# Reordering the last tiles and the four quads of the first up-projection

## The chip, the cores and the metric

The kernel runs on one core of one Trainium2 chip. The metric is the time of one execution on the device in microseconds (us). Five engines of the core take part: PE (TensorE, matrix products), DVE (VectorE), ACT (ScalarE), POOL (GpSimd) and SP (SyncE, which issues nearly all the DMAs). Each works through its own instructions strictly in the order in which they were written, and waits at an instruction until its operands and its destination are free.

## What is computed

A chunked attention with a small memory feeds two feed-forward layers. In the reference, cut to what matters:

```python
def _attn_ref(q, k, v, mem_k, mem_v):          # per chunk of 32 queries, 16 left, 8 right, 8 memory slots
    scores = scale * np.matmul(q_c, k_full.transpose(0, 1, 3, 2))
    ...
    out[:, :, c_start:c_end] = np.matmul(a, v_full)

def _moe_ref(x, w_in, w_out, s, b):            # x: 3072 x 512, w_in: 512 x 2048, w_out: 2048 x 512
    h = x @ w_in
    r = np.maximum(h, 0.0)
    g = s * (r * r) + b
    return g @ w_out

def _moe2_ref(x, w_in, w_out):
    h = x @ w_in
    g = h - np.tanh(h)
    return g @ w_out
```

The change lies in the attention and in `h = x @ w_in` of the first layer ("up 1").

## The kernel before

Every product of two matrices is made of three matmuls, since both operands are split into an upper part (rounded, made by ACT) and a lower part (the rest, made by DVE): upper by upper on L238, lower weights by upper tokens on L239, upper weights by lower tokens on L240. A matmul has 128 x 128 weights and 512 columns.

The tokens stand in six blocks of 512. The work on them goes through these stages:

- **The list** (`START`): attention and the first 36 tiles of up 1, written out by hand as tokens of a letter and a number. `F` is a tile's products (12 matmuls of 512 columns), `r` its relu on ACT, which reads the bank of PSUM, `Q` its square into the group's tile `oa` (on ACT for tiles in `SCALAR_SQUARES`, else on DVE, where it also reads the bank). Tiles share three banks in turn, so tile n+3 can't start before `r` or `Q` of tile n has read its bank. Four tiles are a group; `k` and `K` form its differences in the tile `ob` on DVE (two instructions each), `st` stores `oa` and then `ob` (L621, L622). There are two pairs of `oa` and `ob`, so a group writes into the tiles of the group before the last, once their stores have landed.
- Beside them stand the conversions of the second layer's weights, piece by piece (numbers 0 to 7): `wl` load (1 MB, into the tile `raw`), `ws` scaled on ACT (L245), `wf` filled on DVE (L251, L255), `wd` store, `wc` four sums on DVE (L964, L892), `ww` their store, which frees `raw`. `wr` 4 to 7 (`w1_sums`) form sums of the weights of up 1 for the quads (five instructions on DVE and a store).
- **The plain run**: tiles 36 to 79, with the last units of attention in bursts. `P2_STEPS` places conversions among them, `QUADRANTS` those of the first down-projection's weights (load at the tile that is the key; `begin` on ACT and `end` on DVE at the two tiles in the value), `EXTRAS` the preparation of the quads: `t_sum` and `t_split` form sums of token blocks and split them, `ws_load` and `ws_split` fetch and split the weights' sums.
- **Four quads**: the last two blocks of tokens are done with seven products in place of eight. Each quad has the products P1 to P7 of six matmuls, in three banks. In the code, PE's order is P6, P2, P5, P1 of the next quad, P3, P7 of the next quad, P4. Between products that add up in one bank, ACT copies the bank's state out (`copy`), so P5 waits for `copy(2)` and P3 for `copy(3)`. `add` (DVE) forms three of the four results, `square` squares them, `combos` forms four differences (DVE) and stores. P7, P6, P5 and P3 use the split sums of weights `ws`, P7 first.
- **The first down-projection** (`down1.run`): its entries of 12 matmuls take parts that are loaded from the stores above and split by ACT (L761) and DVE (L762) into the ring.

SP's queue of DMAs holds up all that stand behind a DMA which waits: for its source, or for the tile that it overwrites. The queue's order is that of the code.

Of the kernel before, what the change touches and what calls it, by code (L numbers as in the profile page):

```python
# [27 lines left out]
NB = 512  # L28
# [123 lines left out]
def tile_chunk_attention_two_ffn(  # L152
# [11 lines left out]
    nc = tc.nc  # L164
# [94 lines left out]
    def filled_in_raw(z, raw):  # L259
# [13 lines left out]
    A_T = {"T3": "E0", "T2": "E1", "T1": ("Z2", "Z3"), "T4": ("Z4", "Q2")}  # L273
    A_WORDS, A_WS = ("Z0", "Z1", "Q1", "Q0"), ("E2", "E11", "E4", "E5")
# [17 lines left out]
    Z2 = {("A11", 0): ("E14", 0), ("A11", 1): ("E14", 1), ("A21", 0): "Z0", ("A21", 1): "Z1",  # L292
          ("A22", 0): "Z7", ("A22", 1): "Z8", ("A12", 0): "Z9", ("A12", 1): "Z10"}
# [210 lines left out]
    full = {}  # L504
# [386 lines left out]
    def minus(out, x, y):  # L891
        nc.vector.tensor_tensor(out=out, in0=x, in1=y, op=ALU.subtract)  # L892
# [111 lines left out]
    for token in START.split():  # L1004
        name = token.rstrip("0123456789")
# [86 lines left out]
    class UpQuad:  # L1092
# [57 lines left out]
        def combos(self):  # L1150
            combine(*(t.rearrange("p s b t -> p s (b t)") for t in (self.oa, self.ob)), nc.vector)
# [8 lines left out]
    q = upq[0]  # L1160
# [2 lines left out]
    q.mult("P7")  # L1163
    for s, q in enumerate(upq):
        p, r = upq[s - 1] if s else None, upq[s + 1] if s + 1 < QUADS else None
        q.mult("P6")
        if p:
            p.add(3)
        q.copy(2)
        if s == 0:  # L1170
            t_split("T4")
            ws_load(3)
        if p:
            p.square(3)
        q.mult("P2")
        q.add(1)
        if s == 3:
            down1.weights(0, 0)
        q.square(1)
        if p:  # L1180
            p.combos()
        else:
            up1_combine(21, None)
            up1_store(21)
        if s == 0:
            quads[0].begin()
            quads.append(down1.load_quadrant("E8"))
        if s == 1:
            quads.pop(0).end()
        if s == 2:  # L1190
            quads.pop(0).end()
            down1.load_to(0)
        q.mult("P5")
        q.copy(3)
        q.add(2)
# [208 lines left out]
    q = quads2[0]  # L1404
# [210 lines left out]
```

## Time and profile before

| | |
|---|---|
| time, median of 3 runs | 1059.72 us (1058.91 to 1062.29) |
| the profiled execution's own time | 1061.24 us |
| its span from first to last instruction | 1059.4 us (1.84 us lie around it) |
| PE busy | 1021.9 us, 96% of the span |
| DVE, ACT busy | 809.6 us (76%), 598.7 us (57%) |
| TensorE's granted clock, mean | 0.99 of full speed |
| moved by DMA | 273.12 MB, 258 GB/s |

Times in rows are counted from the span's start. A row's "idle before" is the time for which its engine stood before this instruction, with what ended the wait behind the arrow. PE's matmuls overlap: a busy PE is not a PE at its peak, and the distance between two starts is what one matmul costs.

### The profile page before, as it was taken

Reading aid. Unit: us, or ns where it says so; the run is one execution under the profiler, and the core shown is the slowest. Engines: PE = TensorE matmul, PEld = TensorE weight load, DVE = VectorE, ACT = ScalarE, POOL = GpSimd, SP = SyncE. Lnnn points to the kernel's source line nnn. Section 1 sums busy time; section 2 is a strip of 40 time slices with the busy share of each in tenths; the row PEclk is TensorE's granted clock in tenths of the full one; section 3 lists DMA queues with packets and bytes.
Section 4 is the critical chain, followed back from the end, with each engine's and each line's share of the span. In section 5 each row is a group of like instructions: output and inputs, shape, how many; then the busy total and the mean of one; then the engine's idle time right before and its main releaser. Section 6 shows DMA issues by size and latency. Waiting matters only on the chain.

```text
span 1059.4 us, 15630 instructions
## 1 busy us (share of the span) xinstructions
PE 1021.9 (96%) x6088; PEld 841.5 (79%) x6088; DVE 809.6 (76%) x993; ACT 598.7 (57%) x1098; POOL 12.6 (1%) x53
## 2 busy tenths in 40 slices
PE   7999969999998789999999999999999999999998
PEld 5888758888876568888888888888888888888887
DVE  7998865787566688889878788888888976776654
ACT  8998626657654466566655554454445564444442
POOL 1000000000000000000000000000000000000000
PEclk9999989999998999999999999999999999999999
DMA  8898696898855699787664146665568995556671
GB/s 339 305 329 315 236 405 271 329 343 299 321 217 213 211 382 348 255 313 261 210 200 158 41 189 238 248 239 218 218 249 321 351 375 186 191 189 243 231 264 60
DMA packets 85930, 273.12 MB, mean 258 GB/s; under 512 B 5984, under 2 KB 13408, under 8 KB 75104
## 3 DMA queue, kind: packets, MB, share of 16 engines
q1 hardware_dynamic: 85856, 272.13, 70.0%
q8 instruction: 47, 0.77, 0.3%
q14 instruction: 27, 0.22, 0.1%
HBM read 163.06 MB, written 109.05 MB: 257 GB/s over the span
## 4 chain that ended last, share of the span: by engine, by line
PE 86%; DVE 6%; DMA 3%; ACT 3%; issue 1%; SPq 1%; DVEq 0%; ACTq 0%
PE pb L238 28%; PE pb L239 27%; PE pb L240 27%; DVE ob L626 2%; PE pb L480 1%; DMA o<-oa 1%; PE pb L371 1%; PE pb L443 1%; DMA v<-in_vw_dram 1%; DVE sm L394 1%; DMA qk<-in_qk_dram 1%; DMA part<-o 1%; ACT sm L412 1%; DVE sm L427 0%; ACT r L600 0%
## 5 line engine op out<-in xcount | busy, mean ns | idle before, releaser
L240 PE MATMUL pb<-ringhringl,whl 128*128 128x512 f32 (+1 forms) x680 | 263.2, 387 | 3.4 <-DVE ringhringl L762 3.4
L238 PE MATMUL pb<-ringhringl,whl 128*128 128x512 f32 (+1 forms) x680 | 263.1, 387 | 1.6 <-ACT ringhringl L761 1.6
L239 PE MATMUL pb<-ringhringl,whl 128*128 128x512 f32 (+1 forms) x680 | 262.9, 387 | 0.0
L766 ACT ACTIVATE ringhringl<-part 128x1024 fp32r<-128x1024 f32 x120 | 127.0, 1060 | 148.9 <-PE pb L240 145.7
L767 DVE TENSOR_TENSOR ringhringl<-part,ringhringl 128x1024 fp32r<-128x1024 f32 x120 | 146.8, 1223 | 73.2 <-ACT ringhringl L766 73.0
L240 PEld LDWEIGHTS pb<-ringhringl,whl 128*128 128x128 f32 x680 | 127.7, 188 | 30.1 <-DVE ringhringl L762 4.7
L238 PEld LDWEIGHTS pb<-ringhringl,whl 128*128 128x128 f32 x680 | 127.7, 188 | 28.3 <-ACT ringhringl L761 2.4
L239 PEld LDWEIGHTS pb<-ringhringl,whl 128*128 128x128 f32 x680 | 127.7, 188 | 26.1
L238 PE MATMUL pb<-xh,w 128*128 128x512 f32 (+1 forms) x344 | 135.8, 395 | 9.1 <-DVE oa L614 8.7
L239 PE MATMUL pb<-xh,w 128*128 128x512 f32 (+1 forms) x344 | 133.4, 388 | 0.1
L240 PE MATMUL pb<-xl,w 128*128 128x512 f32 (+1 forms) x344 | 133.3, 387 | 0.0
L239 PE MATMUL pb<-x2hx2l,w 128*128 128x512 f32 x224 | 87.1, 389 | 0.0
L238 PE MATMUL pb<-x2hx2l,w 128*128 128x512 f32 x224 | 87.1, 389 | 0.0
L240 PE MATMUL pb<-x2hx2l,w 128*128 128x512 f32 x224 | 87.1, 389 | 0.0
L238 PEld LDWEIGHTS pb<-xh,w 128*128 128x128 f32 x344 | 65.3, 190 | 25.4 <-DVE oa L614 10.3
L761 ACT ACTIVATE ringhringl<-part,b_c 128x1024 fp32r<-128x1024 f32 x48 | 54.9, 1149 | 38.0 <-PE pb L240 28.4
L600 ACT ACTIVATE r<-pb 128x512 f32<-128x512 f32 x80 | 47.1, 595 | 51.7 <-PE pb L240 50.7
L240 PEld LDWEIGHTS pb<-xl,w 128*128 128x128 f32 x344 | 65.2, 190 | 13.3
L239 PEld LDWEIGHTS pb<-xh,w 128*128 128x128 f32 x344 | 65.3, 190 | 12.7 <-DVE w L570 0.3
L1367 ACT ACTIVATE pb<-oa 128x512 f32<-128x512 f32 x72 | 43.2, 599 | 53.8 <-DVE oa L1359 52.8
L762 DVE SCALAR_TENSOR_TENSOR ringhringl<-part,b_c,ringhringl 128x1024 fp32r<-128x1024 f32 x48 | 61.4, 1282 | 15.6 <-ACT ringhringl L761 15.5
L412 ACT ACTIVATE sm<-sm,nmx 128x96 f32<-128x96 f32 x192 | 69.1, 368 | 4.0 <-DVE nmx L404 4.0
(177 smaller groups left out, 1501.9 us busy)
## 6 DMA issues: line engine op xcount, KB each, us to landing
part<-o SPq DMA_DIRECT2D x84, 512.0 KB, 5.3
part<-o SPq DMA_DIRECT2D x42, 1024.0 KB, 5.9
o<-oa SPq DMA_DIRECT2D x24, 1024.0 KB, 3.9
o<-ob SPq DMA_DIRECT2D x20, 1024.0 KB, 5.8
o<-ob SPq DMA_DIRECT2D x24, 768.0 KB, 5.3
raw<-in_wi_dram SPq DMA_DIRECT2D x16, 1024.0 KB, 6.7
raw<-in_wo_dram SPq DMA_DIRECT2D x16, 1024.0 KB, 8.7
o<-oa SPq DMA_DIRECT2D x20, 768.0 KB, 5.8
```

The source lines that it names most:

```text
L238: nc.tensor.matmul(acc, lhsT=whi, rhs=xhi, start=first, stop=False, skip_group_check=more)
L239: nc.tensor.matmul(acc, lhsT=wlo, rhs=xhi, start=False, stop=False, skip_group_check=more)
L240: nc.tensor.matmul(acc, lhsT=whi, rhs=xlo, start=False, stop=last, skip_group_check=more)
L371: nc.tensor.matmul(score_bank(u, g)[QE * e:QE * (e + 1), KE * (r0 + r):KE * (r0 + r + 1)], lhsT=tq[sl, r, QE * e:QE * (e + 1)], rhs=tk[sl, ...
L412: nc.scalar.activation(out=sm[:, h, :], in_=sm[:, h, :], func=AF.Exp, bias=nmx[:, h:h + 1], scale=1.0, **({"accum_out": sums[:, h:h + 1]} ...
L600: nc.scalar.activation(out=r, in_=up_ps[p], func=AF.Relu)
L626: sub = lambda o, x, y: eng.tensor_tensor(out=o, in0=x, in1=y, op=ALU.subtract)
L761: nc.scalar.activation(out=xh, in_=src, func=AF.Identity, bias=self.bias)
L762: nc.vector.scalar_tensor_tensor(out=xl, in0=src, scalar=self.bias, in1=xh.bitcast(F32), op0=ALU.add, op1=ALU.subtract)
L766: nc.scalar.activation(out=xh, in_=src, func=AF.Copy)
L767: nc.vector.tensor_tensor(out=xl, in0=src, in1=xh.bitcast(F32), op=ALU.subtract)
L1367: nc.scalar.activation(out=self.rs[o], in_=src, func=AF.Tanh)
```

## The change

Three places change; no matmul is added, removed or moved.

**In the list**, the conversion of piece 3 and the sums `wr6` and `wr7` leave it: piece 3 goes to tiles 42 to 50 of the plain run (the later pieces move up to 8 tiles back), the sums to tiles 38 and 41. The steps of piece 0 move to later places in the list. **At the end of the plain run**, the sums of tokens T2 and T4 get tiles of their own and are formed earlier. **In the quads**, splitting the weights is cut in two: the upper part is made before `copy(2)`, the lower part right behind `add(1)`; `combos` is cut in halves, one ahead of P2 and one behind `add(2)`; the conversion (`end`) comes last; square 2 goes from one instruction on DVE to two on ACT. The last quad splits the down-projection's weights at these places, and loads three parts two quads earlier.

```diff
-wr4 r19 r21 F20 ws0 F24 Q19 wr5 r20 E14 F22 r22 qk16 D12 st3 Q20 wf0 wd0 F23 r23 wr6 Q21 ws2 F25 k4
-Q22 wc0 ww0 F26 wl3 Q23 wf2 wd2 K4 r24 r26 F27 st4 D14 k5 r25 K5 Q24 wc2 ww2 F28 Q25 wr7 Q26 ws3 r27
-F29 st5 Q27 wf3 wd3 F30 r29 r28 Q29 wc3 ww3 k6 K6 r30 st6 Q28 F31 F32 X13 Q30 r31 L13 T12 T14 Q31
-r32 k7 K7 Q32 F35 r35 F34 Q35 C12 r34 F33 vv12 Q34 r33 st7 S16 V12 Q33 k8 K8 st8 X12 M16 L12 R16 C14
+wr4 r19 r21 F20 F24 Q19 wr5 r20 E14 F22 r22 qk16 D12 st3 Q20 F23 r23 Q21 ws2 F25 k4 Q22 F26 ws0 Q23
+wf2 K4 r24 r26 F27 wd2 st4 D14 k5 r25 K5 Q24 wc2 F28 Q25 Q26 r27 F29 ww2 st5 Q27 F30 r29 r28 Q29 k6
+K6 r30 st6 Q28 F31 F32 X13 Q30 r31 L13 T12 T14 Q31 r32 k7 K7 Q32 F35 r35 F34 Q35 C12 r34 F33 vv12
+Q34 wf0 r33 st7 wc0 S16 V12 Q33 k8 K8 wd0 ww0 st8 X12 M16 L12 R16 C14
...
-for m, at in ((4, (42, 45, 46, 50)), (5, (50, 53, 54, 58)), (6, (58, 60, 61, 64)), (7, (66, 68, 69, 72))):
+for m, at in ((3, (42, 45, 46, 50)), (4, (50, 53, 54, 57)), (5, (57, 60, 61, 64)), (6, (64, 67, 68, 71)),
+              (7, (71, 74, 75, 78))):
...
     EXTRAS = {
-        71: [(ws_load, 0), (ws_load, 1)], 72: [(t_sum, "T3")], 74: [(t_split, "T3")], 75: [(t_sum, "T2")],
-        76: [(t_split, "T2")], 77: [(t_sum, "T1"), (t_split, "T1")], 78: [(ws_split, 0), (ws_load, 2)],
-        79: [(t_sum, "T4")],
+        38: [(w1_sums, 6)], 41: [(w1_sums, 7)],
+        71: [(ws_load, 0), (ws_load, 1), (t_sum, "T3"), (t_sum, "T2")], 72: [(t_sum, "T1"), (t_split, "T1")],
+        73: [(t_sum, "T4"), (ws_load, 2)], 74: [(t_split, "T3")], 76: [(t_split, "T2")],
+        77: [(t_split, "T4"), (ws_load, 3)], 78: [(ws_high, 0), (ws_low, 0)],
     }
...
-            if o in (0, 1):
+            if o != 3:
                 nc.scalar.activation(out=t, in_=t if o else self.acc(0), func=AF.Relu)
...
         q.mult("P6")
         if p:
             p.add(3)
+            p.square(3)
+        if r:
+            ws_high(s + 1)
         q.copy(2)
...
-        if p:
-            p.square(3)
-        q.mult("P2")
-        q.add(1)
...
         if p:
-            p.combos()
+            p.combos(0)
...
+        q.mult("P2")
+        q.add(1)
...
+        if r:
+            ws_low(s + 1)
+        else:
+            down1.low(0, 0)
+        q.mult("P5")
+        q.copy(3)
+        q.square(1)
+        q.add(2)
+        if p:
+            p.combos(1)
...
-        if r:
-            ws_split(s + 1)
-            r.mult("P1")
-            r.copy(1)
...
         q.mult("P3")
-        q.square(2)
         q.square(0)
-        if s == 1:
-            quads[0].begin()
+        if s in (1, 2):
+            quads.pop(0).end()
...
         if r:
             r.mult("P7")
+        q.square(2)
```

On SP's queue, near the list's end, before (`ws` are the sums of up 1's weights, `w2z` the converted weights, `raw` a load, `o1` the groups' stores):

```order
L981 DMA w1s_5_88<-ws_1706 128x1024
L340 DMA qk_1738<-in_qk_dram 128x1152
L621 DMA o1_0_73<-oa_1426 128x1536
L622 DMA o1_0_73<-ob_1427 128x2048
L958 DMA w2z_0_91<-zw_1691 128x1024
L981 DMA w1s_6_89<-ws_1766 128x1024
L970 DMA w2z_0_91<-raw_1468 128x1024
L544 DMA raw_1808<-in_wi2_dram 128x2048
L958 DMA w2z_2_93<-zw_1774 128x1024
L621 DMA o1_1_74<-oa_1662 128x1536
```

and now, at the same place:

```order
L982 DMA w1s_5_88<-ws_1704 128x1024
L341 DMA qk_1736<-in_qk_dram 128x1152
L622 DMA o1_0_73<-oa_1426 128x1536
L623 DMA o1_0_73<-ob_1427 128x2048
L959 DMA w2z_2_93<-zw_1762 128x1024
L622 DMA o1_1_74<-oa_1662 128x1536
```

Four DMAs between the stores of group 3 (`o1_0_73`) and group 4 (`o1_1_74`) are gone.

On DVE, in the second quad, before (`keep` to `oa` is an `add`, `oa` to `oa` a square, `ob` the differences, `zq` the conversion, `ws` the weights' lower part):

```order
L1140 TENSOR_TENSOR oa_3590<-keep_3556,pb_69 128x2x256
L1148 SCALAR_TENSOR_TENSOR oa_3590<-oa_3590 128x2x256
L1140 TENSOR_TENSOR oa_3659<-keep_3555,pb_69 128x2x256
L626 TENSOR_TENSOR ob_3591<-oa_3590 128x512
L626 TENSOR_TENSOR ob_3591<-oa_3590,ob_3591 128x512
L626 TENSOR_TENSOR ob_3591<-oa_3590 128x512
L626 TENSOR_TENSOR ob_3591<-ob_3591,oa_3590 128x512
L251 TENSOR_SCALAR zq_3601<-zq_3601 128x1024
L255 SCALAR_TENSOR_TENSOR zq_3601<-raw_3449,zq_3601 128x1024
L1140 TENSOR_TENSOR oa_3659<-oa_3659,pb_69 128x2x256
L892 TENSOR_TENSOR ws_3682<-words_3536,ws_3682 128x1024
L1148 SCALAR_TENSOR_TENSOR oa_3659<-oa_3659 128x2x256
```

and now:

```order
L1146 TENSOR_TENSOR oa_3600<-keep_3564,pb_69 128x2x256
L1154 SCALAR_TENSOR_TENSOR oa_3600<-oa_3600 128x2x256
L627 TENSOR_TENSOR ob_3601<-oa_3600 128x512
L627 TENSOR_TENSOR ob_3601<-oa_3600,ob_3601 128x512
L1146 TENSOR_TENSOR oa_3668<-keep_3563,pb_69 128x2x256
L893 TENSOR_TENSOR ws_3655<-words_3432,ws_3655 128x1024
L1146 TENSOR_TENSOR oa_3668<-oa_3668,pb_69 128x2x256
L627 TENSOR_TENSOR ob_3601<-oa_3600 128x512
L627 TENSOR_TENSOR ob_3601<-ob_3601,oa_3600 128x512
L252 TENSOR_SCALAR zq_3590<-zq_3590 128x1024
L256 SCALAR_TENSOR_TENSOR zq_3590<-raw_3523,zq_3590 128x1024
```

The weights' lower part has moved ahead of two differences, the conversion and the second `add`.

On ACT, at the end of the last quad, before (`whl` the down-projection's weights, `ringhringl` the first part's upper half, `oa` from `pb` a copy or a relu out of the bank):

```order
L856 ACTIVATE whl_3805<-zq_2221,sign_105 128x1024
L1145 ACTIVATE oa_3802<-oa_3802 128x2x256
L1146 ACTIVATE oa_3802<-oa_3802 128x2x256
L1136 ACTIVATE oa_3802<-pb_69 128x2x256
L1145 ACTIVATE oa_3802<-pb_69 128x2x256
L1146 ACTIVATE oa_3802<-oa_3802 128x2x256
L856 ACTIVATE whl_3844<-zq_2518,sign_105 128x1024
L761 ACTIVATE ringhringl_3847<-part_3745,b_c_103 128x1024
```

and now:

```order
L857 ACTIVATE whl_3809<-zq_2202,sign_105 128x1024
L1142 ACTIVATE oa_3817<-pb_69 128x2x256
L1151 ACTIVATE oa_3817<-oa_3817 128x2x256
L1152 ACTIVATE oa_3817<-oa_3817 128x2x256
L857 ACTIVATE whl_3840<-zq_2506,sign_105 128x1024
L1151 ACTIVATE oa_3817<-pb_69 128x2x256
L1152 ACTIVATE oa_3817<-oa_3817 128x2x256
L1151 ACTIVATE oa_3817<-oa_3817 128x2x256
L1152 ACTIVATE oa_3817<-oa_3817 128x2x256
L762 ACTIVATE ringhringl_3853<-part_3719,b_c_103 128x1024
```

The copy out of the bank now stands ahead of the first square, and two more instructions (square 2) stand between it and the ring.

## Rows read from the trace of the kernel before

**Rows 1.** By stretch: PE, PEld, DVE, ACT, POOL busy us; clock, DMA share, GB/s.
```profile
120.00:160.00 40.00, 31.11 (x149) 23.96 (x148) 27.00 (x48) 13.27 (x23) 0.00 (x0) 0.87 0.94 374
160.00:200.00 40.00, 39.74 (x370) 32.69 (x369) 24.64 (x36) 24.10 (x75) 0.69 (x3) 1.00 0.75 274
200.00:300.00 100.00, 100.00 (x856) 83.44 (x855) 71.12 (x107) 65.30 (x167) 1.69 (x5) 1.00 0.89 332
307.00:364.00 57.00, 45.64 (x170) 34.26 (x169) 36.24 (x48) 28.38 (x43) 0.00 (x0) 0.91 0.47 167
381.00:1059.00 678.00, 675.29 (x3002) 559.90 (x3000) 527.53 (x588) 349.80 (x426) 0.00 (x0) 1.00 0.65 235
```

**Rows 2.** Waits of PE from 299 to 382 us: total, times, longest.
```profile
PE pb L239 <- DVE ws L892: 5.6, 3, 2.4
PE pb L238 <- ACT oa L1136: 3.6, 2, 2.3
PE pb L240 <- DVE ringhringl L762: 3.4, 3, 2.0
PE pb L238 <- ACT ringhringl L761: 1.6, 2, 0.9
```

**Rows 3.** Timeline of the list's end: start, duration; SP's queue, ACT, DVE, PE.
```profile
130.29 0.33 SPq L544 DMA_DIRECT2D raw<-in_wi_dram  x1
131.15 0.42 SPq L621 DMA_DIRECT2D o<-oa  x1
137.81 0.84 SPq L621 DMA_DIRECT2D o<-oa  x1
...
124.92 1.12 ACT L245 ACTIVATE zw<-raw 128x1024 f32<-128x1024 f32 x1
140.04 1.15 ACT L612 ACTIVATE oa<-r 128x512 f32<-128x512 f32 x2 [11.28 <-DMA o<-oa]
...
126.79 1.23 DVE L255 SCALAR_TENSOR_TENSOR zw<-raw,zw 128x1024 int32<-128x1024 int32 x1
...
140.77 0.80 PE L238 MATMUL pb<-xh,w 128*128 128x512 f32 x1 [7.40 <-DVE oa L614]
150.06 0.50 PE L238 MATMUL pb<-xh,w 128*128 128x512 f32 x1 [1.02 <-DVE oa L614]
```

**Rows 4.** DMA issues of the page: KB each, median us to landing.
```profile
raw<-in_wo_dram SPq DMA_DIRECT2D x16, 1024.0 KB, 8.7
o<-oa SPq DMA_DIRECT2D x20, 768.0 KB, 5.8
```

**Rows 5.** Timeline into and in the quads: ACT, DVE, PE.
```profile
331.59 1.05 ACT L1050 ACTIVATE ws<-words 128x1024 fp32r<-128x1024 f32 x1
334.06 0.63 ACT L1146 ACTIVATE oa<-oa 128x512 f32<-128x512 f32 x1
...
281.39 0.69 DVE L502 TENSOR_TENSOR xl<-pb,xh 128x512 fp32r<-128x512 f32 x1 [0.35 <-ACT xf L511]
285.29 0.70 DVE L251 TENSOR_SCALAR zq<-zq 128x1024 int32<-128x1024 int32 x1 [3.21 <-ACT zq L245]
290.11 0.42 DVE L892 TENSOR_TENSOR raw<-zw 128x256 f32<-128x256 f32 x1
333.04 1.23 DVE L255 SCALAR_TENSOR_TENSOR zq<-raw,zq 128x1024 int32<-128x1024 int32 x1
334.78 1.22 DVE L892 TENSOR_TENSOR ws<-words,ws 128x1024 fp32r<-128x1024 f32 x1
335.92 0.68 DVE L1148 SCALAR_TENSOR_TENSOR oa<-oa 128x512 f32<-128x512 f32 x1
...
308.40 0.39 PE L240 MATMUL pb<-xl,w 128*128 128x512 f32 x1
336.06 0.50 PE L239 MATMUL pb<-thtl,ws 128*128 128x512 f32 x1 [2.43 <-DVE ws L892]
363.65 0.39 PE L240 MATMUL pb<-tl,w 128*128 128x512 f32 x1
```

More of the change, by code (lines that the diff above doesn't have):

```diff
@@ L114 @@
 QUADRANTS = {
-    37: ("E8", 40, 41), 45: ("E9", 48, 49), 53: ("E8", 56, 57), 61: ("E9", 64, 65), 67: ("E8", 70, 71),
-    73: ("E8", 76, 77), 75: ("E9", None, None),
+    37: ("E8", 40, 41), 45: ("E9", 48, 49), 53: ("E8", 55, 56), 59: ("E9", 61, 62), 66: ("E8", 68, 69),
+    73: ("E9", 76, 77), 78: ("E9", None, None),
 }
@@ L268, in tile_chunk_attention_two_ffn @@
     A_RAW = ("E8", "E9")
-    P2_RAW = ("E9", "E8", "E8", "E9", "E8", "E9", "E8", "E9")
+    P2_RAW = ("E9", "E8", "E8", "E8", "E9", "E8", "E9", "E8")
     A_QK, A_V = ("Q0", "Q1", "Q2"), ("Z0", "Z1", "Z2")
@@ L272, in tile_chunk_attention_two_ffn @@
     A_FULL = ("Q0", "Q1")
-    A_T = {"T3": "E0", "T2": "E1", "T1": ("Z2", "Z3"), "T4": ("Z4", "Q2")}
-    A_WORDS, A_WS = ("Z0", "Z1", "Q1", "Q0"), ("E2", "E11", "E4", "E5")
+    A_T = {"T3": "E0", "T2": "E1", "T1": ("Z2", "Z3"), "T4": ("Z4", "Q0")}
+    A_WORDS, A_WS = ("Z0", "Z1", "Q1", "Q2"), ("E2", "E11", "E4", "E5")
     A_OT = (("E14", "E15"), ("E16", "E17"))
@@ L1021, in t_sum @@
     def t_sum(name):
-        f0, f1 = full[0], full[1]
         xh, xl = (t.bitcast(F32) for t in x_t[NBLK - 2])
+        if name in ("T2", "T4"):
+            full[name] = new({"T2": "Z4", "T4": "Q2"}[name], 2 * NB, F32, "t").rearrange("p (c t) -> p c t", c=2)
         plus = lambda out, x, y: nc.vector.tensor_tensor(out=out, in0=x, in1=y, op=ALU.add)
         if name == "T3":
-            minus(f0, f1, f0)
+            minus(full[0], full[1], full[0])
         elif name == "T2":
-            plus(f0, f0, xh[:, 0:2])
-            plus(f0, f0, xl[:, 0:2])
+            plus(full[name], full[0], xh[:, 0:2])
+            plus(full[name], full[name], xl[:, 0:2])
         elif name == "T1":
-            minus(f1, f1, f0)
+            minus(full[1], full[1], full["T2"])
         else:
-            minus(f0, xh[:, 2:4], f0)
-            plus(f0, f0, xl[:, 2:4])
+            minus(full[name], xh[:, 2:4], full["T2"])
+            plus(full[name], full[name], xl[:, 2:4])
     def t_split(name):
-        src = full[name == "T1"]
+        src = full.pop({"T3": 0, "T1": 1}.get(name, name))
         hi, lo = (t.rearrange("p (c t) -> p c t", c=2) for t in pair(A_T[name], 2 * NB, ("th", "tl")))
@@ L1045, in ws_load, with ws_high, ws_low @@
         nc.sync.dma_start(out=w1_words[s], in_=w1s[8 - QUADS + s])
-    def ws_split(s):
-        w, src = new(A_WS[s], 2048, F32R, "ws"), w1_words.pop(s)
+    def ws_high(s):
+        w = ws_hl[s] = new(A_WS[s], 2048, F32R, "ws")
+        nc.scalar.activation(out=w[:, 0:1024], in_=w1_words[s], func=AF.Copy)
+    def ws_low(s):
+        w = ws_hl[s]
         hi, lo = w[:, 0:1024], w[:, 1024:2048]
-        nc.scalar.activation(out=hi, in_=src, func=AF.Copy)
-        minus(lo, src, hi.bitcast(F32))
+        minus(lo, w1_words.pop(s), hi.bitcast(F32))
         ws_hl[s] = tuple(t.rearrange("p (q c m) -> p q c m", q=4, c=2) for t in (hi, lo))
     EXTRAS = {
-        71: [(ws_load, 0), (ws_load, 1)], 72: [(t_sum, "T3")], 74: [(t_split, "T3")], 75: [(t_sum, "T2")],
-        76: [(t_split, "T2")], 77: [(t_sum, "T1"), (t_split, "T1")], 78: [(ws_split, 0), (ws_load, 2)],
-        79: [(t_sum, "T4")],
+        38: [(w1_sums, 6)], 41: [(w1_sums, 7)],
+        71: [(ws_load, 0), (ws_load, 1), (t_sum, "T3"), (t_sum, "T2")], 72: [(t_sum, "T1"), (t_split, "T1")],
+        73: [(t_sum, "T4"), (ws_load, 2)], 74: [(t_split, "T3")], 76: [(t_split, "T2")],
+        77: [(t_split, "T4"), (ws_load, 3)], 78: [(ws_high, 0), (ws_low, 0)],
     }
@@ L1148, in square, with combos @@
                 nc.vector.scalar_tensor_tensor(out=t, in0=t, scalar=0.0, in1=t, op0=ALU.max, op1=ALU.mult)
-        def combos(self):
-            combine(*(t.rearrange("p s b t -> p s (b t)") for t in (self.oa, self.ob)), nc.vector)
+        def combos(self, half):
+            oa, ob = (t.rearrange("p s b t -> p s (b t)") for t in (self.oa, self.ob))
+            combine(oa, ob, nc.vector, half)
+            if half == 0:
+                return
             q, k = divmod(self.n, 2)
@@ L1165, in tile_chunk_attention_two_ffn @@
         p, r = upq[s - 1] if s else None, upq[s + 1] if s + 1 < QUADS else None
+        if s == 2:
+            down1.load_to(2)
         q.mult("P6")
@@ L1168, in tile_chunk_attention_two_ffn @@
             p.add(3)
+            p.square(3)
+        if r:
+            ws_high(s + 1)
         q.copy(2)
-        if s == 0:
-            t_split("T4")
-            ws_load(3)
         if p:
-            p.square(3)
-        q.mult("P2")
-        q.add(1)
-        if s == 3:
-            down1.weights(0, 0)
-        q.square(1)
-        if p:
-            p.combos()
-        else:
-            up1_combine(21, None)
-            up1_store(21)
+            p.combos(0)
+        else:
+            up1_combine(21, 0)
         if s == 0:
@@ L1188, in tile_chunk_attention_two_ffn @@
         if s == 1:
+            quads[1].begin()
+        if s == 3:
+            down1.high(0, 0)
+        q.mult("P2")
+        q.add(1)
+        if s == 3:
+            down1.load_to(3)
+        if r:
[8 more added lines that the diff above has]
+            p.combos(1)
+        else:
+            up1_combine(21, 1)
+            up1_store(21)
+        if r:
+            r.mult("P1")
+            r.copy(1)
+        else:
+            down1.high(0, 1)
+            down1.low(0, 1)
+        q.mult("P3")
+        q.square(0)
+        if s in (1, 2):
             quads.pop(0).end()
         if s == 2:
[L1191 to L1195, printed above, removed]
-        if r:
-            ws_split(s + 1)
-            r.mult("P1")
-            r.copy(1)
-        if s == 3:
-            down1.load_to(3)
-        q.mult("P3")
-        q.square(2)
-        q.square(0)
-        if s == 1:
-            quads[0].begin()
+            down1.sums(0, 0)
+            down1.sums(0, 1)
         if r:
             r.mult("P7")
+        q.square(2)
         if s == 3:
-            down1.weights(0, 1)
             down1.split(0)
@@ L1269, in between1 @@
             upq[-1].square(3)
-            upq[-1].combos()
+            upq[-1].combos(0)
+            upq[-1].combos(1)
         for step in PARTS.get((p, k), ()):
```

## Prediction

> **What bounds the kernel now.** I read the page first (PE busy 96% of the span, DVE 76%, ACT 57%), then busy time by stretch, then PE's waits, then the timelines of the stretches in which PE loses time. In the last long stretch 3002 matmuls start in 678 us [rows 1], 0.226 us each, and PE is full; it is full from 160 to 300 us too. So PE bounds the kernel, and only places where PE stands or is clocked down can give anything back. Three of them lie where the diff works.
>
> The list's end: from 120 to 160 us PE is busy for 31.1 of 40 us at a granted clock of 0.87 [rows 1]. Tile F29 starts at 140.77 after a wait of 7.40 for a square on DVE [rows 3]. That square (Q26) and the one on ACT (Q24, which stood for 11.28 us) write into `oa` of group 6, the tile that group 4's store still reads. SP issued that store at 131.15, behind the load of `raw` at 130.29 [rows 3]; it landed just before 140.04, 8.8 us later, against a median of 5.8 [rows 4]. From 140.77 to the end of the 24 matmuls of F29 and F30 (150.06 less F31's own wait of 1.02) 8.27 us pass, in place of 24 x 0.226 = 5.42: the clock's lower level of 1.2 GHz, after PE had stood, costs another 2.85.
>
> The quads: between the start of the last matmul of the first P1 (308.40) and that of the last P4 (363.65) [rows 5] lie 55.25 us and four quads of 42 matmuls less these six, 162 x 0.226 = 36.6. Lost: 18.6 us. Waits for the weights' lower part are 5.6 of that, waits for `copy` 3.6 [rows 2], the rest smaller waits, restarts and the clock, granted at 0.91 there [rows 1].
>
> The first entries of the down-projection: waits for the ring, 3.4 + 1.6 = 5.0 us [rows 2], with restarts about 5.8. These losses together bound any gain at some 36 us.
>
> **The list's end.** No matmul changes. The relu, `ws`, `wf`, `wd`, `wc`, `ww` of piece 3, its raw load, and the two `w1_sums` with loads and stores leave it. `ws0` now stands on ACT between Q22 and Q23: 1.12 us (the like-shaped instruction at 124.92 [rows 3]), of which I let 0.7 reach PE, so PE gets to F29 at 133.37 + 0.7 = 134.1 (133.37 is 140.77 less 7.40). `wf2` ends at 126.79 + 1.23 = 128.02 [rows 3]; its store goes out at once and group 4's store of `oa` right behind, at 128.45, no longer behind the raw load and with about 1 MB less to move ahead of it. With the median landing of 5.8 [rows 4] it is there at 134.25; DVE is done with `wc2`'s sums by about then, too. Q26 (0.69) lets F29 start at about 135.15: a wait of 1 us, which I take as too short to bring the clock down, since the wait of 1.02 ahead of F31 was followed by a matmul of 0.50 where the wait of 7.40 was followed by one of 0.80 [rows 3]. F31 follows 5.42 later, 140.6; group 5's store (issued at 137.81 before) goes at about 134.9, lands at 140.7, and Q28 lets F31 start at 141.4. Gain 150.06 - 141.4 = **8.7**. Bounds: with a landing of 8.8 once more, F29 waits 3 longer and the gain is 5.8; with no wait at all it is 10.2.
>
> **The plain run.** Two `w1_sums` (about 3 us of DVE each: four halves of 0.42 and a 1024-wide instruction of 1.22 [rows 5]) and one piece more come in. DVE is busy for 24.64 of 40 us from 160 to 200 and for 71 of 100 from 200 to 300 [rows 1]: cost 0, hidden by 15 and 29 us of idle; uncovered it would be up to 6. About 3 MB more to move in 200 to 300 raise 332 GB/s to some 362, below the 374 that the stretch from 120 to 160 reached [rows 1].
>
> **The last tiles.** The sums of T2 and T4 now leave their sources alone, so nothing waits for a split before the next sum; T4's split leaves the first quad. DVE's list from 282.05 (281.39 + 0.69 [rows 5]) to the lower part of the first `ws`: eleven instructions of 1.22, eight differences of 0.69, two fills of 0.70 + 1.23, eight of 0.42 [rows 5] = 26.2, and about 1.4 for ACT's splits: 309.65. P7 of the first quad is due at 308.40 + 0.226 and its second matmul needs that part at 308.85: **0.8** of waiting (bounds 0 and 2.4).
>
> **Inside a quad** (us from the start of its P6; a product is 6 x 0.226 = 1.36, a quad 9.49). ACT: upper part of the next weights 0.2 to 1.25 (1.05 at 331.59 [rows 5]), `copy(2)` to 2.15, needed by P5 at 2.72; `copy(3)` 4.28 to 4.88, needed by P3 at 5.44. DVE: `add(3)` and square 3 to 1.6, first differences to 2.9, `add(1)` to 3.6, the lower part (1.22) to 4.8, needed by the next P7 at 6.8: 2.0 to spare. Before, it stood behind the conversion (333.04) at 334.78, and PE waited 2.43 for it [rows 5]. The `add(2)`, the other differences and the conversion follow and end at 8.8 of 9.49, with nobody waiting. So a quad runs without a wait, at the full clock. In the last quad no P1 stands between P5 and P3, and P3 waits 0.85 for `copy(3)`. New length: 36.6 + 0.8 + 0.85 = 38.3, against 55.25: 16.9. I take off 0.7 for the first conversion, whose `raw` is loaded at about 307 and lands 8.7 later [rows 4]: standing on ACT ahead of `copy(3)`, it can hold P3 (bounds 0 and 1.65). Quad: **gain 16.2**.
>
> Square 2 goes from DVE (0.68 at 335.92) to ACT, where it is two instructions of 0.63 [rows 5]. ACT is busy for 28.4 of 57 us there against DVE's 36.2 [rows 1], so three of the four cost nothing; the last one's 1.26 us stand ahead of the ring and are counted below. The Trainium skill ("ScalarE: Activation LUTs", Rules for kernel authors) says the opposite of the edit: relu and products belong on VectorE, not on ScalarE. By that rule alone the change would lose 4 x (1.26 - 0.68) = 2.3 us and the sum would be 24.1. The rows show the same ratio of costs, but also which engine has time to spare.
>
> **The first down-projection.** Behind the last P3, ACT does square 0 and square 2 (2 x 1.26) and then the ring's upper half (1.05 or a little more), 3.6 in all and 0.7 for hand-overs, less P4's 1.36: PE stands for 2.9; the lower half is 0.75 late behind that. That is 3.65, and 0.7 for an even chance that the clock falls for 1.4 us. The later waits go, since those parts are loaded two quads earlier. Gain 5.8 - 4.35 = **1.45** (bounds -1 and 3).
>
> **Sum.** 8.7 + 16.2 + 1.45 = 26.4. The profiled execution took 1061.2 us (span 1059.4 and 1.8 around it), so 1034.8; it lies 1.5 above the median of 1059.7, so on the median's basis **1033.3**. All bounds at once would be 4.5 us lower, or 8 us higher (14 with the plain run's 6).
>
> **The rivals.**
> A, half of the quads' gain goes to the queue: SP's new order puts the early loads for the down-projection and the converted weights' last stores ahead of group 21's and the quads' stores, and ACT's conversion stands ahead of `copy(3)`. If a load lands after 8.7 us instead of in the time that a quad leaves, each of three quads stands for about 3 us and is clocked down for as long after: 11 us less, 1033.3 + 11 = 1044.5. For it: the load's 8.7 [rows 4] is nearly a quad. Against: only 167 GB/s are moved there [rows 1].
> B, the change does nothing for the quads (the time returns as waits for parts at the down-projection's start): only the list gains, 1059.7 - 8.7 = 1051. Against: PE's waits there are for DVE and ACT, and the loads have room.
> C, slower: the pieces now follow each other in one buffer at tiles 57 to 59, 64 to 66 and 71 to 73, two tiles (5.4 us) apart. SP stands at the load until the earlier store has landed, with the group's stores behind it. From a landing of about 10 us on, a group's squares wait as they did at the list's end, 7.4 + 2.85 + 1.0 = 11 to 12 us each time: 3 x 12 = 36, less 26.4: 1069. Against: a median landing of 5.8 [rows 4], and PE at 100.00 of 100 us there [rows 1], with slack of a group.
>
> **Chances.** Forecast (1028 to 1039) 0.66; A 0.20; B 0.05; C 0.06; below 1028 0.03. The range 1028 to 1045 takes in the forecast's bounds and A and leaves out the rest. A measurement of this kernel tells about 0.3% (3 us) from no change. Faster by more: forecast, A, B and the last, 0.94, less 0.02 for small losses that add up to the gain: 0.92. C gives 0.05 to slower and 0.01 to the same, which is so 0.03.
>
> **What the changed profile would show.** The list: group 4's store issued near 128.5, PE's wait ahead of F29 near 1 us with a clock near 1.0. Quads: no wait for `ws` beyond the first P7's, 9.5 us from P6 to P6, granted clock 1.00. Down-projection: one wait of about 3 us for ACT's ring and few behind. Plain run: still full. Wrong if PE waits for DVE's `oa` between tiles 57 and 76 (C), or for `copy(3)` in each quad (A), or if group 4's landing takes 8.8 us again.

## The result and the profile after

The changed kernel takes 1044.86 us (median of 4 runs, 1044.27 to 1046.08) where the kernel before took 1059.32 beside it: ratio 0.9861, 95% interval 0.9839 to 0.9883. That is 14.5 us faster, where 26.4 were forecast. The profiled execution took 1046.08 us, its span is 1044.2.

Four moments divide the span of the profiled executions, one of each kernel (15.2 us apart): the start of F31, the start of the last matmul of the first P1, that of the last P4, and the end.

| from the moment before to | before | after | gained in this stretch | forecast |
|---|---|---|---|---|
| F31 | 150.06 | 140.74 | 9.3 | 8.7 |
| the first P1's last matmul | 308.40 | 306.14 | -7.1 | 0 |
| the last P4's last matmul | 363.65 | 350.64 | 10.8 | 16.2 |
| the end of the span | 1059.4 | 1044.2 | 2.2 | 1.45 |

So the list gave what was forecast, the plain run took most of it back, and the quads gave two thirds. (Line numbers of the changed kernel are one to nine higher: L239 to L241 are the three matmuls, L601 `r`, L613 and L615 the square on ACT and on DVE, L246 a conversion's first step on ACT, L252 its next on DVE, L893 and L977 differences and sums on DVE, L1142 `copy`, L762 the ring's upper half; L444 are the attention's transposes on PE, L395 its masked scores on DVE.)

The changed kernel by stretch, columns as in [rows 1]:

```profile
120.00:160.00 40.00, 36.91 (x241) 28.98 (x240) 23.12 (x39) 18.79 (x32) 0.00 (x0) 1.00 0.80 322
160.00:200.00 40.00, 38.77 (x307) 31.51 (x306) 32.57 (x51) 24.86 (x86) 1.02 (x4) 1.00 0.84 321
200.00:300.00 100.00, 96.76 (x832) 80.26 (x831) 73.52 (x107) 63.41 (x150) 1.38 (x4) 0.98 0.85 329
```

PE gains 5.8 us from 120 to 160 and the clock is whole there; but from 160 to 300, where it had been full, it now stands for about 4.5 us and the clock is below 1.00 for a while. DVE has 32.57 us to do from 160 to 200 where it had 24.64.

PE's largest waits from 100 to 400 us (total, times, longest):

```profile
PE pb L239 <- ACT oa L1142: 4.8, 1, 4.8
PE pb L444 <- DVE sm L395: 3.8, 6, 1.8
PE pb L239 <- ACT r L601: 2.5, 2, 1.4
PE pb L239 <- ACT ringhringl L762: 1.9, 1, 1.9
PE pb L239 <- DVE oa L615: 0.9, 2, 0.6
PE pb L240 <- DVE ws L893: 0.7, 1, 0.7
```

The 7.4 ahead of F29 has become 0.6 (L615), the three waits for `ws` have become one of 0.7. Two lines are new. One is a single wait for a `copy` in the quads. The other, six waits of the attention's transposes (L444) for the masked scores (`sm`, L395), is PE standing in the bursts of attention at tiles 44, 51 and 58.

The list's end on SP's queue, ACT, DVE and PE (start, duration):

```profile
128.09 0.32 SPq L959 DMA_DIRECT2D w2z<-zw  x1
128.50 0.38 SPq L622 DMA_DIRECT2D o<-oa  x1
...
132.74 1.15 ACT L613 ACTIVATE oa<-r 128x512 f32<-128x512 f32 x2 [3.12 <-DMA o<-oa]
...
126.11 0.69 DVE L252 TENSOR_SCALAR zw<-zw 128x1024 int32<-128x1024 int32 x1 [7.76 <-ACT zw L246]
...
134.37 1.28 DVE L615 TENSOR_TENSOR oa<-pb,r 128x512 f32<-128x512 f32 x2
...
128.69 0.50 PE L239 MATMUL pb<-xh,w 128*128 128x512 f32 x1 [1.05 <-ACT r L601]
135.10 0.50 PE L239 MATMUL pb<-xh,w 128*128 128x512 f32 x1 [0.64 <-DVE oa L615]
140.74 0.50 PE L239 MATMUL pb<-xh,w 128*128 128x512 f32 x1
```

Group 4's store goes out at 128.50 (forecast 128.45), F29 starts at 135.10 (forecast 135.15), and F31 no longer waits. The store landed by 132.74, when Q24 on ACT goes on. Q26 on DVE starts only at 134.37, and not because of that landing: from 126.11 on DVE works through its list without a gap, and Q26 stands in it behind `wc2`'s sums. Each matmul behind a wait runs at 0.50 here, not at the 0.80 that followed the wait of 7.40 [rows 3].

**The first burst**, tile 44, on DVE, SP's queue and PE:

```profile
179.90 1.21 DVE L977 TENSOR_TENSOR ws<-w 128x1024 f32<-128x1024 f32 x1
181.60 1.34 DVE L893 TENSOR_TENSOR ws<-ws 128x256 f32<-128x256 f32 x3
182.86 1.28 DVE L615 TENSOR_TENSOR oa<-pb,r 128x512 f32<-128x512 f32 x2
184.06 0.95 DVE L395 SCALAR_TENSOR_TENSOR sm<-pb,mask_first 128x768 f32<-128x768 f32 x1
...
182.97 0.32 SPq L982 DMA_DIRECT2D w1s<-ws  x1
183.40 0.97 SPq L545 DMA_DIRECT2D raw<-in_wi_dram  x1
...
183.60 1.15 PE L481 MATMUL pb<-pt,v 96*64 96x64 f32 x32 [0.46 <-DVE oa L615]
185.06 0.65 PE L444 MATMUL pb<-ident,sm 64*96 64x64 f32 x16 [0.31 <-DVE sm L395]
```

The `w1_sums` of tile 41 (`ws`) hold DVE from 179.90 to 182.9; two squares follow, then the mask, which PE's transposes wait for. And SP's queue stood at these sums' store: the load of the next piece (`raw`) went out at 183.40, at the very end of the sums.

At the burst of tile 51 it is a load that comes late, and at 58 PE stands longest. From the chain that ended last, then ACT and PE:

```profile
191.72 11.90 DMA raw<-in_wo_dram
...
203.71 1.12 ACT L246 ACTIVATE zq<-raw 128x1024 f32<-128x1024 f32 x1 [2.66 <-DMA raw<-in_wo_dram]
...
210.39 0.65 PE L444 MATMUL pb<-ident,sm 64*96 64x64 f32 x16 [1.05 <-DVE sm L395]
...
236.62 0.65 PE L444 MATMUL pb<-ident,sm 64*96 64x64 f32 x16 [1.77 <-DVE sm L395]
```

The load of a quadrant landed 11.90 us after its issue at 191.72. Its conversion then ran on DVE from 204.86 on, `sums` of piece 3 behind it, and the burst's masks behind those.

**The last quad**, in the chain that ended last (start, duration, what):

```profile
335.15 10.54 DMA o<-oa
346.44 0.79 PE pb L239
347.24 0.43 PE pb L240
```

and on SP's queue and ACT:

```profile
328.07 4.74 SPq L884 DMA_DIRECT2D part<-o  x6
335.15 1.99 SPq L1164 DMA_DIRECT2D o<-oa  x1
337.19 1.41 SPq L1165 DMA_DIRECT2D o<-ob  x1
...
345.80 0.60 ACT L1142 ACTIVATE oa<-pb 128x512 f32<-128x512 f32 x1 [5.15 <-DMA o<-oa]
```

`copy(3)` of the last quad writes the tile `oa` that the second quad used, and that quad's store, issued at 335.15 behind six part loads (three parts in two DMAs each, 3 MB), lands after 10.54 us. P3 then starts at 346.44 after a wait of 4.76, and the clock is at its lower level into the last P4 (0.56 of full speed granted from 346.0 to 349.6): 11 steps take 4.20 us in place of 2.49, another 1.7.

### The profile page after: what moved, and what is told of

It is laid out like the page before. It is cut to its first block, busy times and chain, and to the rows that moved or that the text cites. A ratio compares the mean times of both kernels' runs of the same rounds, so it can differ in the third digit from the quotient of the medians.

```text
span 1044.2 us, 15640 instructions
## 1 busy us (share of the span) xinstructions
PE 1017.2 (97%) x6088; PEld 840.2 (80%) x6088; DVE 805.6 (77%) x989; ACT 604.7 (58%) x1106; POOL 12.2 (1%) x53
## 4 chain that ended last, share of the span: by engine, by line
PE 80%; DVE 8%; DMA 7%; ACT 4%; issue 1%; SPq 0%; ACTq 0%; DVEq 0%
PE pb L239 26%; PE pb L241 26%; PE pb L240 26%; DMA raw<-in_wo_dram 3%; DMA o<-oa 2%; ACT sm L413 1%; DVE ob L627 1%; DVE sm L395 1%; PE pb L372 1%; DVE oa L615 1%; PE pb L481 1%; DVE ws L893 1%; DMA v<-in_vw_dram 1%; PE pb L444 1%; DVE xl L503 1%
## 5 line engine op out<-in xcount | busy, mean ns | idle before, releaser
L239 PE MATMUL pb<-ringhringl,whl 128*128 128x512 f32 (+1 forms) x680 | 263.5, 387 | 1.9 <-ACT ringhringl L762 1.9
L241 PE MATMUL pb<-ringhringl,whl 128*128 128x512 f32 (+1 forms) x680 | 263.5, 387 | 0.4 <-DVE ringhringl L763 0.4
L239 PEld LDWEIGHTS pb<-ringhringl,whl 128*128 128x128 f32 x680 | 128.0, 188 | 28.3 <-ACT ringhringl L762 2.3
L241 PEld LDWEIGHTS pb<-ringhringl,whl 128*128 128x128 f32 x680 | 128.0, 188 | 27.2 <-DVE ringhringl L763 1.0
L239 PE MATMUL pb<-xh,w 128*128 128x512 f32 (+1 forms) x344 | 135.4, 394 | 3.3 <-ACT r L601 2.5
L241 PE MATMUL pb<-xl,w 128*128 128x512 f32 (+1 forms) x344 | 132.6, 385 | 0.0
L239 PE MATMUL pb<-x2hx2l,w 128*128 128x512 f32 x224 | 87.1, 389 | 0.0
L241 PE MATMUL pb<-x2hx2l,w 128*128 128x512 f32 x224 | 87.1, 389 | 0.0
L239 PEld LDWEIGHTS pb<-xh,w 128*128 128x128 f32 x344 | 64.8, 188 | 19.8 <-ACT r L601 3.3
L762 ACT ACTIVATE ringhringl<-part,b_c 128x1024 fp32r<-128x1024 f32 x48 | 54.9, 1151 | 37.1 <-PE pb L241 35.3
L241 PEld LDWEIGHTS pb<-xl,w 128*128 128x128 f32 x344 | 64.9, 189 | 13.3
L601 ACT ACTIVATE r<-pb 128x512 f32<-128x512 f32 x80 | 46.7, 593 | 43.9 <-PE pb L241 43.2
```

What stands on the lines that cost most here:

```text
L239: nc.tensor.matmul(acc, lhsT=whi, rhs=xhi, start=first, stop=False, skip_group_check=more)
L241: nc.tensor.matmul(acc, lhsT=whi, rhs=xlo, start=False, stop=last, skip_group_check=more)
L601: nc.scalar.activation(out=r, in_=up_ps[p], func=AF.Relu)
L762: nc.scalar.activation(out=xh, in_=src, func=AF.Identity, bias=self.bias)
```

## The experiments

The kernel before took 1062 to 1063 us on the chips of these runs, so ratios are compared, not times. The changed kernel was not run again beside these; where a run is compared with it, that goes by its ratio of 0.9861 and by the traces.

**1 and 2. Either part alone.** The kernel before with the new list, pieces, quadrant loads and `w1_sums` places, and the kernel before with the new quads and sums of tokens.

> The kernel before with the new list, conversion pieces, quadrant loads and w1_sums at tiles 38 and 41, but with the old quads and the old sums of tokens. Theory from the traces (the list gives 9.3 us and the plain run takes 7.3 back, because work moved ahead of the attention bursts on DVE and in SP's queue makes PE wait in the bursts at tiles 44, 51 and 58): 1057 to 1058. Rival, as the prediction had it (the plain run hides the moved work): 1050 to 1051.

> The kernel before with the new quads and sums of tokens, but the old list, conversion pieces and quadrant loads. Theory (the quads give 11.0 and the start of the down-projection 2.2 by themselves, the 4.8 us wait for the last copy(3) is the quads' own and stays): 1046 to 1047, with a wait of 4 to 5 us for copy(3). Rival (that wait comes from transfers that the list's change put off to here): the wait is below 1.5 us and the time about 1040.

Measured: the list's part alone 0.9991 (0.9966 to 1.0015), the quads' alone 0.9891 (0.9862 to 0.9920). PE's waits of the first, 100 to 300 us:

```profile
PE pb L444 <- DVE sm L395: 3.5, 6, 1.8
PE pb L239 <- ACT r L601: 3.3, 1, 3.3
PE pb L239 <- DVE oa L615: 0.9, 2, 0.6
```

The list's wait is gone and the bursts wait as in the changed kernel: with this part alone nothing that can be measured is left, against the 0.992 of the prediction's 8.7 us. (The 3.3 for `r` is an earlier store that landed later in this execution, and costs it about 2 us.) With the new quads alone the bursts at 44, 51 and 58 wait for nothing, and the last `copy(3)` still makes PE wait:

```profile
PE pb L238 <- ACT oa L1140: 4.4, 1, 4.4
```

That wait is the quads' own and doesn't come from what the list put off. Both losses are placed. The ratio of 0.9891 is 11 to 12 us; the theory's 11.0 + 2.2 would be 0.9875, inside the interval.

**3. The sums at two other tiles.**

```diff
-        38: [(w1_sums, 6)], 41: [(w1_sums, 7)],
+        61: [(w1_sums, 6)], 63: [(w1_sums, 7)],
...
-        t = new("Z8", 1024, F32, "ws")
+        t = new("Z8" if n < 6 else "Z11", 1024, F32, "ws")
```

> The changed kernel with w1_sums 6 and 7 at tiles 61 and 63 in place of 38 and 41 (in another place of memory). Theory (the sums at tile 41 hold DVE at the burst of tile 44 and, through their store, SP's queue, so that the next loads come late for the burst of tile 51): both bursts take 4.85 us again, gain 3.2, 1041.5 to 1042. Rival 1 (the burst at 51 loses to the extra piece itself): only 1.7, 1043.2. Rival 2 (DVE has too little room anywhere and the loss moves to the burst at 65): 1044.9.

Measured: 0.9875 (0.9848 to 0.9903), no gain. PE's waits from 150 to 300 us say why:

```profile
PE pb L239 <- DVE xl L503: 3.2, 1, 3.2
PE pb L444 <- DVE sm L395: 0.9, 2, 0.7
PE pb L239 <- DVE oa L615: 0.3, 1, 0.3
```

The bursts at 44 and 51 are clean, as the theory had it. But at 63 the sums stand ahead of the burst at 65, and there the second one even waited for the store of the first. PE waits 3.2 at once for `xl` (the lower part of a token block, which DVE makes in the burst), and the clock falls. By its time, rival 2 was right; whether it is the total of DVE's work or the place was open.

**4. Piece 4's sums behind the burst at 58.**

```diff
-for m, at in ((3, (42, 45, 46, 50)), (4, (50, 53, 54, 57)), (5, (57, 60, 61, 64)), (6, (64, 67, 68, 71)),
+for m, at in ((3, (42, 45, 46, 50)), (4, (50, 53, 54, 58)), (5, (57, 60, 61, 64)), (6, (64, 67, 68, 71)),
...
-    37: ("E8", 40, 41), 45: ("E9", 48, 49), 53: ("E8", 55, 56), 59: ("E9", 61, 62), 66: ("E8", 68, 69),
+    37: ("E8", 40, 41), 45: ("E9", 48, 49), 53: ("E8", 55, 56), 60: ("E9", 62, 63), 66: ("E8", 68, 69),
```

> The changed kernel with the sums of piece 4 at tile 58 in place of 57, behind the burst on DVE, and the quadrant load that takes their buffer one tile later. Theory (these four sums stand ahead of the burst's mask on DVE, and the stand of PE then brings the clock down): the burst at 58 loses 2.9 and the clock 1.0 less, 1041.0. Rival (the conversion ahead of them, late because its load landed late, sets the burst): at most 0.5 less, 1044.4 to 1044.9.

Measured: 0.9877 (0.9837 to 0.9918), no gain. The longest wait at 58 falls from 1.77 to 0.31, but two waits for `xl` (2.9 together) appear behind the bursts at 65 and 70. The quadrant's conversion now stands two tiles ahead of the first of these; the second was not followed up. So these sums did stand in the way of the burst at 58, and moving them gave no time. They are not the whole cause either: run 6 leaves them at 57, and the wait falls to 0.5.

**5. The sums in places where DVE is idle.** In the changed kernel DVE is idle for 5.6 us at the list's end, and for 6.0 us right behind the burst at 65:

```diff
-Q34 wf0 r33 st7 wc0 S16 V12 Q33 k8 K8 wd0 ww0 st8 X12 M16 L12 R16 C14
+Q34 wf0 r33 st7 wc0 wd0 ww0 wr6 S16 V12 Q33 k8 K8 st8 X12 M16 L12 R16 C14
...
-        t = new("Z8", 1024, F32, "ws")
+        t = new("Z8" if n < 7 else "Z5", 1024, F32, "ws")
...
-        38: [(w1_sums, 6)], 41: [(w1_sums, 7)],
+        66: [(w1_sums, 7)],
```

> The changed kernel with w1_sums 6 at the list's end (DVE idle 5.6 us there) and 7 at tile 66 (idle 6 us, right behind a burst). The run with both at 61 and 63 freed the bursts at 44 and 51 and lost the same at 65. Theory (it is only the place ahead of a burst that costs): no new loss, bursts at 44 and 51 take 4.85 us, the one at 58 loses about 1 in place of 2.9: ratio 0.981 to 0.983. Rival (the stretch has too much work for DVE or the DMA queues as a whole, so that some burst loses it anyway): 0.985 to 0.988 and a new wait at 58, 65 or 70.

Measured: 0.9792 (0.9771 to 0.9814). PE's waits from 150 to 300 us:

```profile
PE pb L444 <- DVE sm L395: 0.9, 2, 0.7
PE pb L239 <- DVE oa L615: 0.3, 1, 0.3
```

No burst took the loss over. DVE does as much as in the changed kernel, so it is the place ahead of a burst that cost, not the amount. (The edit also gives sums 7 another place of memory. That isn't the cause: in the changed kernel nothing waited from 150 to 300 us for the store that reads the old one.) Part of the gain came back later: the first P7 waited 1.73 for `ws` in place of 0.69, and the last `copy(3)` cost 5.71 in place of 4.76.

**6. Only the second of them.** Sums 6 stay at tile 38, only sums 7 go from 41 to 66 (and to the other place of memory, as in run 5).

> The changed kernel with w1_sums 6 still at tile 38 and only 7 moved, to tile 66. Theory (the sums at tile 41 alone make both losses: their 3 us stand ahead of the burst at 44 on DVE, and their store holds the loads behind it on SP's queue, so that a conversion comes late into the burst at 51): both bursts take 4.85 us, ratio as with both moved, 0.979 to 0.981. Rival (the burst at 51 is late by the extra piece's traffic, and moving 6 off helped it): the burst at 51 still waits 1 us or more, ratio 0.982 to 0.984.

Measured: 0.9812 (0.9776 to 0.9847), and the bursts at 44 and 51 wait for nothing; the one at 58 waits 0.7. On SP's queue the load that had gone out at 183.40, at the end of those sums, is no longer behind them, and the quadrant's conversion no longer waits for its load:

```profile
PE pb L444 <- DVE sm L395: 0.7, 2, 0.5
...
180.36 0.33 SPq L545 DMA_DIRECT2D raw<-in_wi_dram  x1
...
191.02 0.42 SPq L545 DMA_DIRECT2D raw<-in_wo_dram  x1
...
200.40 1.14 ACT L246 ACTIVATE zq<-raw 128x1024 f32<-128x1024 f32 x1
```

PE is 0.9 us later here than in the changed kernel from the list's end on. So the piece's load went out 3.9 us earlier against the burst, and the quadrant's 1.6 earlier; that one had landed by 200.40, within 9.4 us rather than 11.90. From F31 to the first P1's last matmul it is 159.6 us (159.5 to 159.7 in runs 5, 8, 9 and 10), where the changed kernel took 165.4 (164.8 and 165.0 in runs 7 and 1, with the sums at 41 too) and the kernel before 158.3: five instructions and a store at one tile explain 5.8 of the 7.1 us, all of the waits at 44 and 51 and most of that at 58.

**7. The part loads behind the store.**

```diff
-        if s == 2:
-            down1.load_to(2)
         q.mult("P6")
...
             up1_store(21)
+        if s == 2:
+            down1.load_to(2)
```

> The changed kernel with the three early part loads of the down-projection (3 MB) issued behind the second quad's stores in place of in front of them. Theory (those loads fill the DMA queues ahead of the store of the oa tile that the last quad's copy(3) overwrites, and the store lands 8 to 10 us after its issue): the store lands in about 5 us, copy(3) waits below 1 us, PE's wait of 4.8 and the 1.9 of lower clock behind it go, less about 1 that comes back as a wait for parts: 0.9800 to 0.9815 of the kernel before, where the changed kernel had 0.9861. Rival (copy(3) is late because the store is issued late, behind DVE's differences): wait above 3 us, ratio 0.985 to 0.987.

Measured: 0.9784 (0.9762 to 0.9805). SP's queue, ACT and PE in the last quad:

```profile
334.02 0.46 SPq L1164 DMA_DIRECT2D o<-oa  x1
337.08 5.29 SPq L884 DMA_DIRECT2D part<-o  x8
...
340.59 0.60 ACT L1142 ACTIVATE oa<-pb 128x512 f32<-128x512 f32 x1 [1.08 <-PE pb L241]
341.24 0.50 PE L239 MATMUL pb<-xh,ws 128*128 128x512 f32 x1 [0.69 <-ACT oa L1142]
343.89 0.40 PE L241 MATMUL pb<-tl,w 128*128 128x512 f32 x1
346.83 0.50 PE L239 MATMUL pb<-ringhringl,whl 128*128 128x512 f32 x1 [2.55 <-ACT ringhringl L762]
```

The store is issued only 1.1 us earlier, at 334.02, and `copy(3)` at 340.59 doesn't wait for it any more, only for PE: it landed within 6.6 us of its issue, not after 10.5. So the loads that were queued ahead of it made it late, not the moment of its issue. (With them in front, the first of the quad's two `oa` stores also went out late, at 332.92 rather than 328.40, because SP was issuing. No run separates that from the loads' bytes.) From the first P1's last matmul (305.26) to the last P4's are 38.63 us; the prediction had 38.3 for that stage, in which it had not counted the store. The ratio is below the theory's 0.9800 to 0.9815, whose lower end the interval still holds. PE waits 2.55 for the ring, where the prediction had 2.9.

**8. Both edits**, those of runs 5 and 7.

> The two edits of the runs before together. Theory (two separate losses): the gains add up, ratio 0.975 to 0.977. Rival (one of them only moves the loss): 0.981 or above.

Measured: 0.9748 (0.9729 to 0.9766), 1035.83 us. The gains add up: two separate losses. In the spans of the profiled executions the edits give 5.6 and 5.1 us alone and 10.9 together; by the ratios 0.008 and 0.007 alone and 0.011 together, which agrees within the intervals.

**9. Square 2 of the last quad on DVE**, on top of both.

```diff
-            if o != 3:
+            if o != 3 and (o, self.s) != (2, QUADS - 1):
```

> The same two edits, and square 2 of the last quad on DVE in one instruction in place of ACT in two. Theory (of the squares moved to ACT only the last one's 1.26 us lies on the path, ahead of the ring's upper half): PE's wait for the ring falls by 0.6 to 1.3 us, ratio 0.001 below that of the run before. Rival (the ring waits for its part or for DVE): no difference.

Measured: 0.9742 (0.9721 to 0.9763): not to be told from run 8. PE's wait for the ring's upper half falls from 2.5 to 1.4, as the theory has it, but in this execution the first P7 waited 1.9 for `ws` in place of 0.5:

```profile
303.24 0.50 PE L240 MATMUL pb<-thtl,ws 128*128 128x512 f32 x1 [1.91 <-DVE ws L893]
...
344.17 0.50 PE L239 MATMUL pb<-ringhringl,whl 128*128 128x512 f32 x1 [1.36 <-ACT ringhringl L762]
```

Runs 5 and 10 have that wait for `ws` too, run 8 has not: a quadrant's conversion ahead of it waited on ACT for its load in runs 5, 9 and 10 (1.2 to 1.6) and not in run 8. The mechanism is shown, its worth of 1.1 us is below what these runs can tell.

**10. `ws0` out of the way.** On top of that, `ws0` goes behind `r26`, where ACT stood idle.

> The kernel with later part loads, sums 6 and 7 in idle places and the last square 2 on DVE, and in the list ws0 behind r26 in place of in front of Q23. Theory (F29's start is set by the landing of group 4's store, not by ACT): PE's wait of 1.05 ahead of F27 goes and comes back ahead of F29, which waits 1.6 to 1.8 in place of 0.65; time unchanged, 0.973 to 0.976. Rival (ACT is what sets the start of F29, as far as its r27 and Q24 stand behind ws0): 1.0 us less, and F29 still waits 0.65.

Measured: 0.9740 (0.9698 to 0.9781), 1034.32 us. The wait of 1.05 ahead of F27 is gone, and F29 shows where it went:

```profile
134.74 0.50 PE L239 MATMUL pb<-xh,w 128*128 128x512 f32 x1 [1.70 <-DVE oa L615]
```

The wait ahead of F29 is 1.70 in place of 0.66, so ACT doesn't set its start. The landing of group 4's store, which the theory named, doesn't either: Q24 on ACT goes on at 132.40, so the store has landed by then, and Q26 starts at 134.00, because DVE's list runs without a gap from 125.75 to there. That list starts when `ws2` is done on ACT, and `ws2` stands behind a square that waited until 122.93 for an earlier group's store. The three kernels of runs 8 to 10 are faster than the kernel before by 2.5% and, by their ratios, than the changed kernel by 1.1%; among them no order can be told.

## Why the prediction came out as it did

The time lies inside the range, 0.14 us below its upper end, and 11.6 us above the forecast. That it lies inside is luck: the range went up to 1045 for the sake of rival A, whose mechanism did not come. The point forecast failed by two of its steps, each worth 5 to 7 us; the others held.

**The list's end** held in its sum: 9.3 us against 8.7, the store's issue and the start of F29 within 0.1 us of the working. The way there was in part another. The store landed 4.2 us after its issue rather than 5.8, and F29 waited for DVE's list, which the working had only in passing ("DVE is done with `wc2`'s sums by about then, too"); that both terms fell at the same moment was luck. So taking `wr7` away from in front of Q26 counted as well as the earlier store: in the kernel before it held DVE to 137.4. `ws0` reached PE with 1.05 rather than 0.7, and run 10 shows that this had no price. F31 lost its wait altogether.

**The plain run** failed: "cost 0, hidden by 15 and 29 us of idle". The idle time of a stretch was counted, and not its place. In a burst PE waits for DVE within one or two tiles, and DVE takes its list in order; 3 us of sums two tiles ahead of a burst can't use idle time that comes behind it. The uncovered price of "up to 6" was in the text, and 7.1 was paid, because the loss went on past the burst at 44: a quadrant's load went out 1.6 us later against the burst than in run 6 and landed after 11.90 us rather than within 9.4, its conversion came into the burst at 51, and behind the longest stand, at 58, the clock fell (0.93 of full speed from 220 to 240 us). Run 6 shows the place of sums 7 to be the cause of 5.8 of the 7.1. The way by which it reached 51, through SP's queue, is what the rows say; no run moved the store alone. The other 1.2 us were not followed up.

**Inside a quad** held for three quads: no wait for `ws` beyond the first P7's (0.7 measured, 0.8 forecast), no wait for `copy(2)`. It failed in the last: "P3 waits 0.85 for `copy(3)`", where it waited 4.76 and lost 1.7 more by the clock. The working knew the engines' order of that `copy` and left out that it writes a tile whose store must have landed. The early part loads had been credited as a gain at the down-projection's start, without a price for what stands behind them on the queue. Run 7, with the loads behind the store, has 0.69 and 38.63 us where the step had 0.85 and 38.3. The 0.7 that was taken off for a conversion waiting on its load was not needed: in the changed kernel ACT did wait 0.85 for that load, but `copy(3)` behind it ended at 313.60, ahead of P3's start at 314.16.

**The down-projection's start** held in kind: one wait for the ring (1.91, forecast 2.9; P4 began at the lower clock, which may have given ACT time, and in run 7, where it did not, the wait is 2.55), the later waits gone, 2.2 us against 1.45.

**The rivals.** A has nearly the measured time (1044.5 in the text, though its own terms, 1033.3 + 11, give 1044.3) but not its reason: it did name early loads ahead of the quads' stores, but had three quads stand for 3 us each, and the loss is one stand in the last quad and three bursts in the plain run. B and C did not come: no group's squares wait between tiles 57 and 76. By the rule of the Trainium skill ("ScalarE: Activation LUTs", Rules for kernel authors) that relu and products belong on VectorE, the prediction priced the four moved squares at 2.3 us. Run 9 shows 1.1 us less of waiting for the one square that lies on the path, and no difference in the time. That the rows show the rule's "same ratio of costs" goes too far: they have 1.26 against 0.68, a ratio of 1.9 in f32, where that section of the Trainium skill names up to about 3 in bf16.

## What to carry to other kernels

Here idle time of an engine that works in order hid moved work only where it lay ahead of the next instruction for which PE waited: look at the one or two tiles in front of each such place, and put the work right behind it. For each transfer that is issued earlier, ask which store stands behind it on the queue and who overwrites that store's source next. A wait that is removed upstream of another limit comes back there (run 10): find out which engine's list or which landing sets the next start, and when two fall together, read both.

## What the runs showed that was not expected

A store of `oa` landed 10.54 us after its issue when six loads of 512 KB had been issued just ahead of it, and within 6.6 when they were behind it; its own issue took 1.99 us on SP in place of 0.46. The median landing of such a store (384 KB) is 4.8 us in the changed kernel.

Stands of PE differ in what follows, and their length alone doesn't tell which. Behind waits of 1.05 and 1.70 in the list, and of 1.73 and 1.74 ahead of the first P7 (runs 5 and 10), the next matmuls started every 0.23 us, at full rate. Behind waits of 1.73 and 1.77 in bursts (run 7 at 51, the changed kernel at 58), and behind 1.91 ahead of the first P7 (run 9, five matmuls later), some started every 0.43 us, the lower level of the clock. Behind the waits of 3.22 (run 3), 4.76 and 7.40, 7 to 13 matmuls did.
